# Two score units per TensorE mode switch, q and k transposes in two groups of four banks, q and k loaded by head halves

## The chip, the cores and the metric

The kernel runs on one core of one Trainium2 chip. The metric is the device time of one execution in microseconds (us), as the median of several runs. Before the change it is 365.46 us (364.68 to 366.66, 4 runs). Runs of one kernel differ by some tenths of a per cent, those of the changed kernel and some of its variants by up to 1.5%; a verdict "faster" or "slower" is given beyond 2%.

## The reference

Eight batches of attention with eight heads, 576 positions and head width 64, in a causal window of 128 with a linear position bias, followed by a two-layer network over all 4608 tokens:

```python
scores = q @ k.T / sqrt(64)                    # per batch and head
bias   = -slope[h] * |i - j|;  mask = (0 <= i - j < 128)
attn   = softmax(where(mask, scores + bias, -1e9))
x      = (attn @ v), heads side by side        # 4608 x 512
h      = x @ w_in                              # 512 -> 2048
out    = (h * cos(h)) @ w_out                  # 2048 -> 512, float32
```

## The kernel before

Everything is recorded in program order by a helper that derives the semaphore waits. Each engine runs its own list strictly in the order recorded. If TensorE's next instruction must wait, everything recorded behind it waits too.

The work is a chain of "chunks" of 512 tokens. For chunk c, TensorE does 16 groups of four first-layer matmuls (`moe1`; ScalarE makes the cosine, VectorE the product), with the q,k transposes of batch c+1 between them. Then comes the attention of batch c+1, whose chain over ScalarE and VectorE is long, so 64 second-layer matmuls of chunk c (`moe2_steps`) are dealt out between its pieces as filler.

```python
HB = [0, 1, 2, 3, 4, 5]                 # PSUM banks of the first layer; second layer: 6, 7
...
def qk_transposes(banks, engs):         # 8 steps: (half of the heads) x (q, k) x (two parts)
    ...                                 # one step: up to 10 transposes into one bank,
                                        # then one copy out of it, ScalarE or VectorE
...
def scores(b, u, n): banks = [2 * (n % 2), 2 * (n % 2) + 1]; ...   # keys 64 rows deep
def pv(b, u, n): ...                    # banks 4, 5; the tail unit "t" takes both
def norm(b, u, n): ...                  # VectorE: reciprocal, multiply
def x_back(b, u, n, eng): ...           # transposes the result back, eng copies it to xT
...
def attention(b, fill, plan):
    lead, part, last = plan
    take(lead)                          # take(n): n filler matmuls
    for j in range(2):
        scores(b, us[j], j)
        exps(b, us[j], j)
    mask(b, us[0])
    for j in range(n + 2):              # n = 9 units; unit 0 of batches 1..7 is the tail "t"
        take(part[0] if j < n else last)
        if 2 <= j:      x_back(b, us[j - 2], j - 2, "act")
        if j + 2 < n:   scores(b, us[j + 2], j + 2); exps(b, us[j + 2], j + 2)
        if j < n:       take(part[1]); pv(b, us[j], j)
        if j + 1 < n:   mask(b, us[j + 1])
        if j < n:       norm(b, us[j], j)
    for s in it: s()                    # what is left of the filler
...
for c in range(NCH):
    if c < B - 1:
        steps = iter(qk_transposes([6, 7], ["dve", "act"]))
        for fc in range(NFC):           # NFC = 16
            moe1(c, fc)
            if fc % 2 == 1:
                next(steps)()
        ...                             # loads of batch c + 2
        attention(c + 1, moe2_steps(c), (8, (2, 3), 3))
```

The transposes of q and k (64 columns wide, 128*64 in the traces), the scores and the tail's transposes back (64 rows deep, 64*128) use the array in halves; all other matmuls use all of it (128*128). "Mode switch" here means going from one to the other.

The softmax here doesn't subtract the row's maximum and nothing guards it: scores larger than these inputs give would overflow.

## Time and profile before

| | us |
|---|---|
| first-layer matmuls of chunk 0 begin (end of the prologue) | 30.62 |
| first period (chunk 0 to chunk 1) | 41.14 |
| each of the following six periods | 39.13 |
| the rest (last two chunks) | 58.76 |
| span of the profiled execution | 365.33 |

The first period is 2.0 us longer because of TensorE's clock. The trace records which share of the full clock was granted: here full from 14.61 us, half from 18.02 to 35.09, then full. Before its first record a trace says nothing, and views show full there; the distance between matmuls tells which clock it was.

The page of the kernel before, busy time by engine and then shares of the chain that ended last:

```profile
PE 341.4 (93%) x2912; PEld 164.6 (45%) x2912; DVE 233.1 (64%) x446; ACT 234.5 (64%) x352; POOL 61.3 (17%) x89
...
PE 79%; ACT 10%; DVE 6%; DMA 2%; issue 1%; POOL 1%; ACTq 0%; DVEq 0%; POOLq 0%
```

TensorE is busy 93% of the span and is 79% of the chain. So the question of any change is what TensorE does, and what it waits for.

The next lines are TensorE's timeline of the kernel before in the first-layer part of one period. Columns: start in us, length in us, engine, line of the program, operation, output and inputs, shapes, count. Lengths of matmuls overlap, since they are pipelined, so I read start to start.

```profile
71.77 1.89 PE L505 MATMUL ps<-xT,w_inb 128*128 128x512 bf16 x8
73.59 0.47 PE L290 MATMUL ps<-ident,qrows 128*64 128x128 bf16 x10
73.99 1.90 PE L505 MATMUL ps<-xT,w_inb 128*128 128x512 bf16 x8
```

Eight first-layer matmuls take 1.82 us until the transposes begin, where eight at the steady 0.216 us take 1.73: the entry costs 0.09. From matmul to matmul in the trace, the last full matmul before a transpose takes 0.309 us instead of 0.216, the first gap between two pairs of transposes 0.077 instead of 0.053, and the last transpose before a full matmul 0.151 instead of 0.056. One pair of switches costs about 0.21 us. A period has 16 pairs.

The same view at the start of the attention. L528 is the filler, L333 the tail scores, L342 the other scores:

```profile
89.40 1.90 PE L528 MATMUL ps<-w_outb,gT 128*128 128x512 bf16 x8
91.23 0.41 PE L333 MATMUL ps<-qt,kt 64*128 64x64 bf16 x16
91.48 0.33 PE L342 MATMUL ps<-qt,kt 64*128 64x256 bf16 x4
91.74 0.60 PE L528 MATMUL ps<-w_outb,gT 128*128 128x512 bf16 x2
92.96 0.39 PE L342 MATMUL ps<-qt,kt 64*128 64x256 bf16 x6 [0.62 <-ACT ptail L357]
```

The eight leading filler matmuls stand before the first scores. The third score unit waits 0.62 us, at 92.96, for the tail's exponential to free its banks.

TensorE's waits in the whole execution. Columns: engine, output, line, what it waited for; then us in total, times, longest:

```profile
PE ps L342 <- ACT ptail L357: 4.4, 7, 0.6
```

This line is that wait, once in each of seven periods. All waits of a period together are about 1.0 us.

### The profile page before, as it was taken

Reading aid. Unit: us, or ns where it says so; the run is one execution under the profiler, and the core shown is the slowest. Engines: PE = TensorE matmul, PEld = TensorE weight load, DVE = VectorE, ACT = ScalarE, POOL = GpSimd, SP = SyncE. Lnnn points to the kernel's source line nnn. Section 1 sums busy time; section 2 is a strip of 40 time slices with the busy share of each in tenths; the row PEclk is TensorE's granted clock in tenths of the full one; section 3 lists DMA queues with packets and bytes.
Section 4 is the critical chain, followed back from the end, with each engine's and each line's share of the span. In section 5 each row is a group of like instructions: output and inputs, shape, how many; then the busy total and the mean of one; then the engine's idle time right before and its main releaser. Section 6 shows DMA issues by size and latency. Waiting matters only on the chain.

```text
span 365.3 us, 7057 instructions
## 1 busy us (share of the span) xinstructions
PE 341.4 (93%) x2912; PEld 164.6 (45%) x2912; DVE 233.1 (64%) x446; ACT 234.5 (64%) x352; POOL 61.3 (17%) x89
## 2 busy tenths in 40 slices
PE   0688999999999999999999999999999999999996
PEld 0453445544454445444544455444544454444442
DVE  1683767577666766675857676776657675754431
ACT  5684786577757786678657875777567765843400
POOL 8860051003400150006000420015000000000000
PEclk9955999999999999999999999999999999999999
DMA  7999979105910193109910691039110011001012
GB/s 114 183 207 206 142 107 125 54 29 66 158 59 31 22 160 75 57 2 135 118 59 0 82 144 58 31 51 160 47 55 0 0 59 60 0 4 56 29 59 86
DMA packets 55648, 28.25 MB, mean 77 GB/s; under 512 B 38720, under 2 KB 51008, under 8 KB 55616
## 3 DMA queue, kind: packets, MB, share of 16 engines
q0 software_dynamic: 50432, 18.36, 44.8%
q1 hardware_dynamic: 5184, 9.44, 6.9%
q8 instruction: 23, 0.38, 0.4%
q14 instruction: 9, 0.07, 0.1%
HBM read 36.70 MB, written 9.44 MB: 126 GB/s over the span
## 4 chain that ended last, share of the span: by engine, by line
PE 79%; ACT 10%; DVE 6%; DMA 2%; issue 1%; POOL 1%; ACTq 0%; DVEq 0%; POOLq 0%
PE ps L505 33%; PE ps L528 30%; PE ps L290 5%; PE ps L342 5%; ACT cos L511 3%; ACT L357 2%; DMA krows<-in_k_dram 2%; PE ps L414 2%; ACT ptail L357 2%; PE ps L473 2%; PE ps L417 1%; ACT kt L303 1%; DVE kt L306 1%; DVE ob L533 1%; DVE gT L514 1%; DVE p L380 1%
## 5 line engine op out<-in xcount | busy, mean ns | idle before, releaser
L528 PE MATMUL ps<-w_outb,gT 128*128 128x512 bf16 x576 | 151.4, 380 | 0.0
L505 PE MATMUL ps<-xT,w_inb 128*128 128x512 bf16 x576 | 138.5, 384 | 0.2 <-ACT xT L487 0.2
L511 ACT ACTIVATE cos<-ps,halfpi 128x512 f32<-128x512 f32 x144 | 98.9, 688 | 52.2 <-PE ps L505 47.7
L514 DVE TENSOR_TENSOR gT<-ps,cos 128x512 bf16<-128x512 f32 x144 | 99.5, 692 | 50.7 <-ACT cos L511 50.7
L505 PEld LDWEIGHTS ps<-xT,w_inb 128*128 128x128 bf16 x576 | 52.6, 98 | 62.2 <-issue 2.4
L528 PEld LDWEIGHTS ps<-w_outb,gT 128*128 128x128 bf16 x576 | 45.6, 97 | 39.6 <-issue 4.4
L366 ACT ACTIVATE p<-ps 128x768 bf16<-128x768 f32 (+1 forms) x64 | 57.6, 915 | 6.2 <-PE ps L342 6.2
L487 ACT ACTIVATE xT<-ps 128x256 bf16<-128x256 bf16 (+3 forms) x80 | 28.9, 363 | 48.5 <-PE ps L473 42.8
L533 DVE COPY ob<-ps 128x512 f32<-128x512 f32 x36 | 24.9, 691 | 34.4 <-PE ps L528 34.4
L380 DVE TENSOR_TENSOR p<-p,emask 128x768 bf16<-128x768 bf16 (+1 forms) x64 | 39.5, 616 | 1.1 <-ACT p L366 0.9
L210 POOL DMA_DIRECT2D qrows<-in_q_dram x16 | 10.1, 640 | 172.4 <-PE ps L290 171.6
L218 POOL DMA_DIRECT2D vp<-in_v_dram x40 | 34.0, 888 | 0.0
L342 PE MATMUL ps<-qt,kt 64*128 64x128 bf16 (+1 forms) x320 | 24.6, 248 | 5.4 <-ACT ptail L357 4.4
L444 DVE TENSOR_TENSOR xnat<-ps,rec 128x256 bf16<-128x256 f32 x64 | 27.2, 425 | 2.2
L414 PEld LDWEIGHTS ps<-vp,p 128*128 128x128 bf16 x256 | 18.3, 100 | 17.4 <-ACT xT L487 8.4
L414 PE MATMUL ps<-vp,p 128*128 128x65 bf16 x256 | 23.1, 198 | 2.2 <-DVE rec L443 0.8
L290 PE MATMUL ps<-ident,qrows 128*64 128x128 bf16 x288 | 15.0, 239 | 8.8 <-DMA qrows<-in_q_dram 8.8
L417 PE MATMUL ps<-vp,p 128*128 128x65 bf16 x192 | 21.1, 198 | 0.0
L473 PE MATMUL ps<-ident,xnat 128*128 128x128 bf16 x128 | 18.6, 230 | 1.4 <-DVE xtail L435 1.2
L290 PEld LDWEIGHTS ps<-ident,qrows 128*64 128x64 bf16 x288 | 10.0, 119 | 21.0 <-issue 12.3
L473 PEld LDWEIGHTS ps<-ident,xnat 128*128 128x128 bf16 x128 | 12.3, 101 | 14.9 <-DVE xtail L435 1.4
L342 PEld LDWEIGHTS ps<-qt,kt 64*128 64x128 bf16 x320 | 11.4, 96 | 16.4 <-ACT ptail L357 7.8
(42 smaller groups left out, 196.7 us busy)
## 6 DMA issues: line engine op xcount, KB each, us to landing
out_dram<-ob SPq DMA_DIRECT2D x36, 256.0 KB, 2.0
qrows<-in_q_dram POOLq DMA_DIRECT2D x16, 288.0 KB, 5.0
krows<-in_k_dram POOLq DMA_DIRECT2D x16, 288.0 KB, 5.1
vp<-in_v_dram POOLq DMA_DIRECT2D x32, 128.0 KB, 6.3
w_inb<-in_moe_w_in_dram POOLq DMA_DIRECT2D x4, 512.0 KB, 10.6
w_outb<-in_moe_w_out_dram POOLq DMA_DIRECT2D x4, 512.0 KB, 19.9
vp<-in_v_dram POOLq DMA_DIRECT2D x8, 64.0 KB, 5.7
```

What stands on the lines that cost most here:

```text
L218: op("pool", lambda e, t=t, rows=rows: e.dma_start(vp[b % 2][0:rows, t, :, 0:64], v[b, :, 128 * t:128 * t + rows, :].rearrange("h p d -> p ...
L290: ins = e.transpose(dst[64 * x:64 * x + 64, 128 * (j - j0):128 * (j - j0) + 128], qB[which][:, 2 * pl + x, 64 * j:64 * j + 64], ident[:, :])
L342: ins = e.matmul(ps[:, banks[x], c0:c1], keys_ap(x, pr, kc), query_ap(x, pr, qb, 128 * nb), start=True, stop=True)
L366: op("act", lambda e: e.activation(P[i][:, :, lo:512], ps[:, 2 * slot:2 * slot + 2, lo:512], ACTF.Exp, scale=0.125), w=[("B", 2 * slot), ( ...
L380: op("dve", lambda e: e.tensor_tensor(P[i][:, :, lo:512], P[i][:, :, lo:512], EM[:, 2 * pr:2 * pr + 2, lo:512], ALU.mult), r=[("P", i), (" ...
L414: ins = e.matmul(o, P[i][:, x, d0:d0 + 128], V[:, kc, h, 0:65], start=True, stop=not two)
L473: ins = e.transpose(dst[:, 128 * r:128 * r + 128], xnat[n % NX][:, 128 * r:128 * r + 128], ident[:, :])
L487: op("act", lambda e, o=o, i=i: e.activation(o, i, ACTF.Copy), w=[("B", bank)] + keys)
L505: ins = e.matmul(ps[:, bank, :], w_in[:, kc, 128 * fc:128 * fc + 128], xT[:, kc, r0:r0 + CH], start=(kc == 0), stop=(kc == NPAIR - 1))
L511: op("act", lambda e: e.activation(cosb[ci][:, :], ps[:, bank, :], ACTF.Sin, bias=halfpi[:, 0:1]), r=["halfpi"], w=[("B", bank), ("cos", ci)])
L514: op("dve", lambda e: e.tensor_tensor(gT[gi][:, fc, :], ps[:, bank, :], cosb[ci][:, :], ALU.mult), r=[("cos", ci)], w=[("B", bank), ("g", ...
L528: op("pe", lambda e: e.matmul(ps[:, bank, :], gT[gi][:, fc, 128 * t:128 * t + 128], w_out[:, fc, :], start=(fc == 0), stop=(fc == NFC - 1) ...
```

## The change

The intent is to save mode switches. The eight transpose groups of a batch become two groups of four banks, two score units are computed in one visit, the PSUM banks are dealt out anew for that (four instead of six for the first layer), and q and k come in halves of the heads, so that work on the first batch can begin earlier.

```diff
-        HB = [0, 1, 2, 3, 4, 5]
+        HB, SB, UB, OB = [0, 1, 2, 3], [4, 5, 6, 7], [2, 3], [0, 1]
     # first layer; scores and transposes; value products; second layer
...
-        def load_qk(which, src, b):
+        def load_qk(which, src, b, pl):        # one half of the heads
...
-        def attention(b, fill, plan):
+        def attention(b, fill, plan, x_eng):
+            ng = (n + 1) // 2                  # groups of two units
+            for j in members(0): scores(b, us[j], j)
+            for j in members(0): exps(b, us[j], j)
+            for j in members(0): mask(b, us[j])
+            for g in range(ng + 1):
+                before, after, between = plan(g)
+                take(before)
+                for j in members(g - 1): x_back(b, us[j], j, x_eng(j))
+                for j in members(g + 1): scores(b, us[j], j)
+                for j in members(g + 1): exps(b, us[j], j)
+                take(after)
+                ahead = list(members(g + 1))
+                for i, j in enumerate(members(g)):
+                    if i: take(between)
+                    pv(b, us[j], j); norm(b, us[j], j)
+                    if i < len(ahead): mask(b, us[ahead[i]])
...
-                steps = iter(qk_transposes([6, 7], ["dve", "act"]))
+                group = [qk_transposes(pl, SB, ["act", "dve", "act", "dve"]) for pl in range(2)]
                 for fc in range(NFC):
                     moe1(c, fc)
-                    if fc % 2 == 1:
-                        next(steps)()
+                    for pl in range(2):
+                        if fc == 1 + 7 * pl:
+                            for tp, cp in group[pl]: tp()      # transposes only
+                        elif fc in [3 + 7 * pl, 4 + 7 * pl, 6 + 7 * pl, 7 + 7 * pl]:
+                            group[pl].pop(0)[1]()          # one copy
...
-                attention(c + 1, moe2_steps(c), (8, (2, 3), 3))
+                attention(c + 1, moe2_steps(c),
+                          lambda g: ((20, 4, 3), (5, 3, 3), (5, 3, 3), (5, 3, 3), (5, 1, 0),
+                                     (4, 0, 0))[g], lambda j: "act")
```

At the 2nd and 9th first-layer group four banks of transposes are issued, and their copies follow one by one in the `elif` branch. In the first batch the change transposes the first half of the heads before the attention and the second half inside it. Not shown: the first batch takes its units in another order and has VectorE make every fourth copy of `x_back`, and there are four buffers for the exponentials instead of three.

More of the change, by code (lines that the diff above doesn't have):

```diff
@@ L177, in bass_alibi_sliding__then__act_gcu_kernel @@
         EMt = sb("emtail", [128, H, 128])
-        NP = 3
+        NP = 4
         P = [sb(f"p{i}", [128, 2, 512]) for i in range(NP)]
@@ L210, in load_qk @@
                 fns.append(lambda e, g=g: e.dma_start(
-                    qB[which][64 * g:64 * g + 64, :, :],
-                    src[b, 4 * g:4 * g + 4, :, :].rearrange("h (s j) d -> s h (j d)", j=9)))
-            op("pool", fns, w=[("qB", which)], dma=f"ld{which}")
+                    qB[which][64 * g:64 * g + 64, 2 * pl:2 * pl + 2, :],
+                    src[b, 4 * g + 2 * pl:4 * g + 2 * pl + 2, :, :].rearrange(
+                        "h (s j) d -> s h (j d)", j=9)))
+            op("pool", fns, w=[("qB", which, pl)], dma=f"ld{which}{pl}")
         def load_v(b, order=range(NBLK)):
@@ L271, in masks, with qk_transposes @@
                    r=[("EM", h) for h in range(x, H, 2)], w=["EMt"])
-        def qk_transposes(banks, engs):
+        def qk_transposes(pl, banks, engs):
             out_ = []
             n = 0
-            for pl in range(2):
-                for which in ("q", "k"):
-                    for (j0, j1) in ((0, 5), (5, 9)):
-                        def step(pl=pl, which=which, j0=j0, j1=j1, n=n):
-                            bank = banks[n % len(banks)]
-                            nj = j1 - j0
-                            dst = ps[:, bank, :].bitcast(BF16)[:, 0:nj * 128]
-                            def tp(e):
-                                ins = None
-                                for j in range(j0, j1):
-                                    for x in range(2):
-                                        ins = e.transpose(
-                                            dst[64 * x:64 * x + 64,
-                                                128 * (j - j0):128 * (j - j0) + 128],
-                                            qB[which][:, 2 * pl + x, 64 * j:64 * j + 64],
-                                            ident[:, :])
-                                return ins
-                            op("pe", tp, r=[("qB", which), "ident"], w=[("B", bank)])
-                            o = tr[which][:, :].rearrange("p (g l t) -> p g l t", g=2, l=2)[
-                                :, :, pl, 0:576].rearrange("p g (s j) -> p g s j", j=9)[
-                                :, :, :, j0:j1]
-                            i = dst.rearrange("p (j g s) -> p g s j", j=nj, g=2)
-                            key = ("tr", which, pl, j0)
-                            if engs[n % len(engs)] == "act":
-                                op("act", lambda e: e.activation(o, i, ACTF.Copy),
-                                   w=[("B", bank), key])
-                            else:
-                                op("dve", lambda e: e.tensor_copy(o, i), w=[("B", bank), key])
-                        out_.append(step)
-                        n += 1
@@ new lines, in qk_transposes, with tp, f, cp @@
+            for which in ("q", "k"):
+                for (j0, j1) in ((0, 5), (5, 9)):
+                    bank = banks[n % len(banks)]
+                    nj = j1 - j0
+                    dst = ps[:, bank, :].bitcast(BF16)[:, 0:nj * 128]
+                    def tp(which=which, j0=j0, j1=j1, bank=bank, dst=dst):
+                        def f(e):
+                            ins = None
+                            for j in range(j0, j1):
+                                for x in range(2):
+                                    ins = e.transpose(
+                                        dst[64 * x:64 * x + 64,
+                                            128 * (j - j0):128 * (j - j0) + 128],
+                                        qB[which][:, 2 * pl + x, 64 * j:64 * j + 64],
+                                        ident[:, :])
+                            return ins
+                        op("pe", f, r=[("qB", which, pl), "ident"], w=[("B", bank)])
+                    def cp(which=which, j0=j0, j1=j1, nj=nj, bank=bank, dst=dst, eng=engs[n]):
+                        o = tr[which][:, :].rearrange("p (g l t) -> p g l t", g=2, l=2)[
+                            :, :, pl, 0:576].rearrange("p g (s j) -> p g s j", j=9)[
+                            :, :, :, j0:j1]
+                        i = dst.rearrange("p (j g s) -> p g s j", j=nj, g=2)
+                        key = ("tr", which, pl, j0)
+                        if eng == "act":
+                            op("act", lambda e: e.activation(o, i, ACTF.Copy),
+                               w=[("B", bank), key])
+                        else:
+                            op("dve", lambda e: e.tensor_copy(o, i), w=[("B", bank), key])
+                    out_.append((tp, cp))
+                    n += 1
@@ L318, in units @@
             if b == 0:
-                return [(pr, G) for G in range(2) for pr in (0, 2, 1, 3)] + [("t", None)]
+                return [(pr, G) for p0 in range(2) for G in range(2) for pr in (p0, p0 + 2)] + [
+                    ("t", None)]
             return [("t", None)] + [(pr, G) for pr in range(NPAIR) for G in range(2)]
@@ L323, in scores @@
             slot = n % 2
-            banks = [2 * slot, 2 * slot + 1]
+            banks = SB[2 * slot:2 * slot + 2]
             def f(e):
@@ L352, in exps @@
             slot = n % 2
+            banks = SB[2 * slot:2 * slot + 2]
+            held = [("B", x) for x in banks]
+            src_ = ps[:, banks[0]:banks[0] + 2, :]
             if u[0] == "t":
@@ L357, in exps @@
                 op("act", lambda e: e.activation(
-                    Pt[i][:, 0:1024], ps[:, 2 * slot:2 * slot + 2, :].rearrange("p a b -> p (a b)"),
-                    ACTF.Exp, scale=0.125),
-                   w=[("B", 2 * slot), ("B", 2 * slot + 1), ("Pt", i)])
+                    Pt[i][:, 0:1024], src_.rearrange("p a b -> p (a b)"), ACTF.Exp, scale=0.125),
+                   w=held + [("Pt", i)])
                 return
@@ L365, in exps @@
             lo = 0 if u[1] else 128
-            op("act", lambda e: e.activation(P[i][:, :, lo:512], ps[:, 2 * slot:2 * slot + 2, lo:512],
+            op("act", lambda e: e.activation(P[i][:, :, lo:512], src_[:, :, lo:512],
                                              ACTF.Exp, scale=0.125),
-               w=[("B", 2 * slot), ("B", 2 * slot + 1), ("P", i)])
+               w=held + [("P", i)])
         def mask(b, u):
@@ L384, in ubanks @@
         def ubanks(u, n):
-            return [4, 5] if u[0] == "t" else [4 + n % 2]
+            return UB if u[0] == "t" else [UB[n % 2]]
         def pv(b, u, n):
@@ L397, in f @@
                             h = 2 * pr + x
-                            o = ps[:, 4 + x, 65 * pr:65 * pr + 65]
+                            o = ps[:, UB[x], 65 * pr:65 * pr + 65]
                             c0 = 512 * x + 128 * pr
@@ L428, in norm @@
             if u[0] == "t":
-                U = ps[0:64, 4:6, 0:260].rearrange("p x (k c) -> p x k c", c=65)
+                U = ps[0:64, UB[0]:UB[0] + 2, 0:260].rearrange("p x (k c) -> p x k c", c=65)
                 rv = rc[0:64, 0:8].rearrange("p (x k) -> p x k", x=2)
@@ L432, in norm @@
                 op("dve", lambda e: e.reciprocal(rv, U[:, :, :, 64]),
-                   w=[("B", 4), ("B", 5), ("rec", n % 2)])
+                   w=[("B", UB[0]), ("B", UB[1]), ("rec", n % 2)])
                 for x in range(2):
@@ L437, in norm @@
                         rv[:, x, :, None].broadcast_to([64, 4, 64]), ALU.mult),
-                       r=[("rec", n % 2)], w=[("B", 4 + x), ("xtl",)])
+                       r=[("rec", n % 2)], w=[("B", UB[x]), ("xtl",)])
                 return
@@ L523, in moe2_steps @@
                 tg = 4 * c + t
-                bank = 6 + tg % 2
+                bank = (OB if c < B - 1 else SB)[tg % 2]
                 oi = tg % NOB
@@ L550, in take, with members @@
                         s()
-            lead, part, last = plan
             us = units(b)
             n = len(us)
-            take(lead)
-            for j in range(2):
+            ng = (n + 1) // 2
+            def members(g):
+                return range(2 * g, min(2 * g + 2, n)) if 0 <= g < ng else ()
+            for j in members(0):
                 scores(b, us[j], j)
+            for j in members(0):
                 exps(b, us[j], j)
-            mask(b, us[0])
-            for j in range(n + 2):
-                take(part[0] if j < n else last)
-                if 2 <= j:
-                    x_back(b, us[j - 2], j - 2, "act")
-                if j + 2 < n:
-                    scores(b, us[j + 2], j + 2)
-                    exps(b, us[j + 2], j + 2)
-                if j < n:
-                    take(part[1])
+            for j in members(0):
+                mask(b, us[j])
@@ new lines, in attention @@
+            for g in range(ng + 1):
+                before, after, between = plan(g)
+                take(before)
+                for j in members(g - 1):
+                    x_back(b, us[j], j, x_eng(j))
+                for j in members(g + 1):
+                    scores(b, us[j], j)
+                for j in members(g + 1):
+                    exps(b, us[j], j)
+                take(after)
+                ahead = list(members(g + 1))
+                for i, j in enumerate(members(g)):
+                    if i:
+                        take(between)
@@ L568, in attention @@
                     pv(b, us[j], j)
-                if j + 1 < n:
-                    mask(b, us[j + 1])
-                if j < n:
                     norm(b, us[j], j)
+                    if i < len(ahead):
+                        mask(b, us[ahead[i]])
+                for j in ahead[len(members(g)):]:
+                    mask(b, us[j])
             for s in it:
                 s()
-        load_qk("q", q, 0)
-        load_qk("k", k, 0)
-        constants()
+        for pl in range(2):
+            load_qk("q", q, 0, pl)
+            load_qk("k", k, 0, pl)
+            if pl == 0:
+                constants()
@@ L580, in bass_alibi_sliding__then__act_gcu_kernel @@
         load_v(0)
         masks()
-        for s in qk_transposes([4, 5, 6, 7], ["dve", "act"]):
-            s()
+        first = qk_transposes(0, UB + OB, ["dve", "act", "dve", "act"])
+        for tp, cp in first:
+            tp()
+            cp()
         for u in range(4):
             load_w_in(u)
-        load_qk("q", q, 1)
-        load_qk("k", k, 1)
+        load_qk("q", q, 1, 0)
+        load_qk("k", k, 1, 0)
+        attention(0, [lambda s=s: (s[0](), s[1]())
+                      for s in qk_transposes(1, OB + UB, ["dve", "act", "dve", "act"])],
+                  lambda g: (0, 2, 2) if g == 0 else (0, 0, 0),
+                  lambda j: "dve" if j % 4 == 3 else "act")
@@ L588, in bass_alibi_sliding__then__act_gcu_kernel @@
+        load_qk("q", q, 1, 1)
+        load_qk("k", k, 1, 1)
         for u in range(4):
             load_w_out(u)
-        load_v(1)
-        attention(0, [], (0, (0, 0), 0))
+        load_v(1, (3, 4, 0, 1, 2))
         for c in range(NCH):
             if c < B - 1:
-                steps = iter(qk_transposes([6, 7], ["dve", "act"]))
+                group = [qk_transposes(pl, SB, ["act", "dve", "act", "dve"]) for pl in range(2)]
                 for fc in range(NFC):
                     moe1(c, fc)
-                    if fc % 2 == 1:
-                        next(steps)()
+                    for pl in range(2):
+                        if fc == 1 + 7 * pl:
+                            for tp, cp in group[pl]:
+                                tp()
+                        elif fc in [3 + 7 * pl, 4 + 7 * pl, 6 + 7 * pl, 7 + 7 * pl]:
+                            group[pl].pop(0)[1]()
@@ L599, in bass_alibi_sliding__then__act_gcu_kernel @@
                 if c + 2 < B:
-                    load_qk("q", q, c + 2)
-                    load_qk("k", k, c + 2)
+                    for pl in range(2):
+                        load_qk("q", q, c + 2, pl)
+                        load_qk("k", k, c + 2, pl)
                     load_v(c + 2)
-                attention(c + 1, moe2_steps(c), (8, (2, 3), 3))
+                attention(c + 1, moe2_steps(c),
+                          lambda g: ((20, 4, 3), (5, 3, 3), (5, 3, 3), (5, 3, 3), (5, 1, 0),
+                                     (4, 0, 0))[g], lambda j: "act")
```

## The prediction

> **What bounds the kernel now.** TensorE issue. The page has PE 93% busy (DVE 64%, ACT 64%); the chain of waits is 79% PE. The timeline shows seven equal periods of 39.1 us (71.77 to 110.91), one per batch: 17.6 us of first-layer matmuls with the q,k transposes between them, 21.5 us of attention filled with 64 second-layer matmuls. A 512-column matmul issues every 0.216 us. Real PE waits in a period are only about 1.0 us: 0.69 for the first tail exponential (after a 1.28 us table load on ACT), 0.33 at a value product.
>
> **What a mode switch costs (PE timeline, start to start).** A full matmul before a 64-wide one: 0.309 us instead of 0.216; the first gap inside the group 0.077 instead of 0.053; leaving, 0.151 instead of 0.056. About 0.21 us a pair. The Trainium skill ("TensorEngine Tiling (Array Packing)", Key Properties) says that changing the tiling mode drains the engine; the trace agrees. Pairs per period: 16 before (8 transpose groups, 8 score visits), 8 after (2 and 6: a full-array transpose now separates the 64-row tail transpose from the scores). Saved: 8 x 0.21 = 1.7 us. If both old waits vanish too: 2.7 us a period, a floor near 36.4.
>
> **What the change adds.** New PE waits in each period, since PE is in order:
> - A. The second transpose group (after matmul group 8) needs its last bank, freed by a DVE copy queued behind the product of group 7. Matmuls begin to product ended is 2.47 us, copy 0.8: about 1.0 us wait.
> - B. The scores of the first two units now come before the lead of second-layer matmuls (before: 8 matmuls, 1.7 us, first). The tail unit needs the last key copy, on DVE behind the product of group 14: free about 3.3 to 3.8 us after that group began, PE arrives at 1.8. Wait 1.5 to 2.0 us.
> - C. The filler plan asks for 70 matmuls of 64. With 20 in the lead, nothing is left after the third-last step: the last unit's product waits for ACT's copy out of its bank (about 0.6), its transpose back for reciprocal and multiply (0.85), and in three of seven periods the next first-layer matmul for the last copy (0.8).
> - E. The tail unit holds both value banks; its normalization takes 1.1 to 1.3 us on DVE, but only 3 matmuls (0.65) stand before the next unit's product: about 0.7.
> - D. Transposes back: 5 matmuls (1.08 us) against a chain of 1.2: 0.4 together.
> Four first-layer banks suffice: a bank is held 2.5 us, reused after 3.46.
>
> Sum: 5.5 to 6 us of waits against 2.7 saved, about +3 us a period, +21 in seven.
>
> **Prologue.** ACT's masks end at 9.6 us and DVE's tail mask at 10.2, so half loads landing earlier save only to there: first scores at about 12 instead of 14.8. First-layer matmuls start 2 to 3 us earlier than 30.6. The last 59 us unchanged.
>
> **Prediction: 383 us, range 369 to 397.** Chances: faster by over 2% 0.07, within 2% 0.11, slower by over 2% 0.82.
>
> **Right or wrong.** Right: half as many 0.309/0.151 gaps, periods near 42 us, PE waits at the places of A to E. Wrong: periods of 37 to 38 us without them: then I misread what covers them.
> **Other risk.** The PE clock was halved (18.0 to 35.1 us) where PE worked thinly; waits B and C might trip this in each period, costing more.

## More of the kernel before

Where the interval of a ratio straddles that limit, the verdict is "unclear".

## The result, and the profile after

The changed kernel takes 397.84 us (393.44 to 398.77, 4 runs). The ratio to the kernel before is 1.086, with a 95% interval of 1.077 to 1.095: slower. Ratios here are the mean time of one kernel's fast runs over that of the other's of the same rounds, so they are not quite the ratio of the medians quoted.

| us | before | after | difference |
|---|---|---|---|
| prologue | 30.62 | 33.94 | +3.3 |
| seven periods together | 275.9 | 298.7 | +22.8 |
| of these, each late period | 39.13 | 42.10 | +3.0 |
| the rest | 58.76 | 58.78 | 0 |
| span of the profiled execution | 365.3 | 391.4 | +26.1 |

The prologue of the changed kernel ran at half clock throughout: the clock records begin at 37.24 us with full clock, and until then first-layer matmuls stand 0.427 us apart instead of 0.216. That of the kernel before had full clock for 3.4 us and then half, so the +3.3 compares nearly, but not quite, the same clock. Half clock until 37.24 also lengthens the first period here (44.37 us; the next two take 43.16 and 42.76).

The page of the changed kernel, the same two lines:

```profile
PE 337.0 (86%) x2912; PEld 169.8 (43%) x2912; DVE 225.9 (58%) x448; ACT 225.7 (58%) x350; POOL 79.6 (20%) x121
...
PE 66%; DVE 18%; ACT 11%; issue 4%; POOL 1%; ACTq 0%; POOLq 0%; DVEq 0%
```

TensorE is busy a little less in all, 337.0 instead of 341.4 us, over a longer span. Its share of the chain fell from 79% to 66%, and VectorE's rose from 6% to 18%. TensorE did not get more work; it waits more.

TensorE's waits of the changed kernel, with the columns as before:

```profile
PE ps L336 <- DVE kt L308: 12.5, 7, 1.8
PE ps L478 <- DVE xnat L449: 12.1, 21, 0.8
...
PE ps L290 <- DVE kt L308: 5.6, 7, 0.8
PE ps L419 <- DVE xtail L440: 4.4, 7, 0.6
...
PE ps L510 <- ACT xT L492: 1.6, 3, 0.7
```

All five are new or longer than before. The three lines with a count of seven happen once in each period. Of the 21 waits on `DVE xnat`, seven (3.7 us) lie in the first batch's attention and two in each period. The last line is of the first three periods only. I call the waits by the letters of the prediction.

TensorE's timeline of the changed kernel in the first-layer part of a period (L510 first layer, L290 transposes). Wait A is the one at 217.20:

```profile
206.34 1.89 PE L510 MATMUL ps<-xT,w_inb 128*128 128x512 bf16 x8
208.16 0.69 PE L290 MATMUL ps<-ident,qrows 128*64 128x128 bf16 x18
208.68 0.67 PE L290 MATMUL ps<-ident,krows 128*64 128x128 bf16 x18
209.28 6.22 PE L510 MATMUL ps<-xT,w_inb 128*128 128x512 bf16 x28
215.43 0.69 PE L290 MATMUL ps<-ident,qrows 128*64 128x128 bf16 x18
215.96 0.45 PE L290 MATMUL ps<-ident,krows 128*64 128x128 bf16 x10
217.20 0.41 PE L290 MATMUL ps<-ident,krows 128*64 128x128 bf16 x8 [0.80 <-DVE kt L308]
217.55 1.68 PE L510 MATMUL ps<-xT,w_inb 128*128 128x512 bf16 x7
```

Each visit now transposes four banks at one switch. But the last eight transposes of the second visit wait 0.80 us (0.96 start to start above the normal gap) for a VectorE copy (`kt L308`): it frees the bank that the first visit used last, and on VectorE it stands behind the product of group 7.

The same view at the start of the attention, with waits B and E (L336 tail scores, L533 filler, L419 value products):

```profile
221.23 2.54 PE L510 MATMUL ps<-xT,w_inb 128*128 128x512 bf16 x11
225.55 0.41 PE L336 MATMUL ps<-qt,kt 64*128 64x64 bf16 x16 [1.79 <-DVE kt L308]
225.78 0.35 PE L345 MATMUL ps<-qt,kt 64*128 64x256 bf16 x4
226.06 4.49 PE L533 MATMUL ps<-w_outb,gT 128*128 128x512 bf16 x20
...
232.34 0.81 PE L533 MATMUL ps<-w_outb,gT 128*128 128x512 bf16 x3
233.78 0.25 PE L419 MATMUL ps<-vp,p 128*128 128x65 bf16 x3 [0.63 <-DVE xtail L440]
```

B: the tail scores come right after the first-layer matmuls and wait 1.79 us for the last copy of the transposed keys. E: the value product at 233.78 waits 0.63 us for the tail unit's normalization, because the tail holds both value banks. In the kernel before, five filler matmuls and a score unit stood between these two.

The end of the same batch, with wait C (L478 transposes back; two rows of the last value product are shown, at 247.16 and 247.38):

```profile
245.54 1.03 PE L533 MATMUL ps<-w_outb,gT 128*128 128x512 bf16 x4
246.41 0.64 PE L478 MATMUL ps<-ident,xnat 128*128 128x128 bf16 x4
247.16 0.20 PE L419 MATMUL ps<-vp,p 128*128 128x65 bf16 x1
...
247.38 0.19 PE L422 MATMUL ps<-vp,p 128*128 128x65 bf16 x1
248.31 0.29 PE L478 MATMUL ps<-ident,xnat 128*128 128x128 bf16 x2 [0.74 <-DVE xnat L449]
248.44 1.24 PE L510 MATMUL ps<-xT,w_inb 128*128 128x512 bf16 x5
```

All 64 filler matmuls are gone at 246.4. From there to the next chunk at 248.44, TensorE has only fourteen short transposes and matmuls in 2 us. It waits about 0.3 us before the last value product and 0.9 us after it. D is the rest of the waits on `DVE xnat`: at 243.27 the second transpose back of a middle group comes 0.63 us late, at 246.77 another 0.24.

From the start-to-start gaps of this late period (206.34 to 248.44) the sum is A 0.96, B 1.86, C 1.17, D 0.87, E 0.80, together 5.7 us. Without them the period would be 36.4 us. The mode switches are saved as planned: counted in the traces, a late period has 8 pairs instead of 16 (at the q,k transposes 2 entries instead of 8, with 0.309 us each). The saving is simply smaller than the waits.

### The profile page after: what moved, and what is told of

It is laid out like the page before. It is cut to its first block, busy times and chain, and to the rows that moved or that the text cites. A ratio compares the mean times of both kernels' runs of the same rounds, so it can differ in the third digit from the quotient of the medians.

```text
span 391.4 us, 7083 instructions
## 1 busy us (share of the span) xinstructions
PE 337.0 (86%) x2912; PEld 169.8 (43%) x2912; DVE 225.9 (58%) x448; ACT 225.7 (58%) x350; POOL 79.6 (20%) x121
## 4 chain that ended last, share of the span: by engine, by line
PE 66%; DVE 18%; ACT 11%; issue 4%; POOL 1%; ACTq 0%; POOLq 0%; DVEq 0%
PE ps L533 28%; PE ps L510 21%; ACT cos L516 7%; DVE gT L519 5%; PE ps L345 4%; PE ps L290 3%; DVE xnat L449 3%; PE ps L419 3%; PE ps L478 3%; DVE kt L308 2%; DVE xtail L440 2%; DVE p L385 1%; PE ps L422 1%; DVE qt L308 1%; DVE ob L538 1%
## 5 line engine op out<-in xcount | busy, mean ns | idle before, releaser
L533 PE MATMUL ps<-w_outb,gT 128*128 128x512 bf16 x576 | 142.3, 380 | 0.0
L510 PE MATMUL ps<-xT,w_inb 128*128 128x512 bf16 x576 | 132.3, 383 | 1.6 <-ACT xT L492 1.6
L516 ACT ACTIVATE cos<-ps,halfpi 128x512 f32<-128x512 f32 x144 | 95.4, 688 | 49.0 <-PE ps L510 45.8
L510 PEld LDWEIGHTS ps<-xT,w_inb 128*128 128x128 bf16 x576 | 54.9, 98 | 67.4 <-ACT xT L492 2.1
L533 PEld LDWEIGHTS ps<-w_outb,gT 128*128 128x128 bf16 x576 | 49.5, 97 | 51.7 <-issue 4.4
L210 POOL DMA_DIRECT2D qrows<-in_q_dram x32 | 19.7, 630 | 182.9 <-PE ps L290 182.1
L448 DVE RECIPROCAL rec<-ps 128x4 f32<-128x4 f32 x64 | 11.5, 180 | 33.0 <-PE ps L422 32.9
L478 PE MATMUL ps<-ident,xnat 128*128 128x128 bf16 x128 | 18.0, 233 | 12.6 <-DVE xnat L449 12.1
L419 PE MATMUL ps<-vp,p 128*128 128x65 bf16 x256 | 23.1, 200 | 6.2 <-DVE xtail L440 4.4
L419 PEld LDWEIGHTS ps<-vp,p 128*128 128x128 bf16 x256 | 19.0, 101 | 19.1 <-issue 8.4
L345 PE MATMUL ps<-qt,kt 64*128 64x128 bf16 (+1 forms) x320 | 20.8, 253 | 3.3 <-DVE kt L308 2.6
L210 POOL DMA_DIRECT2D krows<-in_k_dram x32 | 19.6, 636 | 2.6 <-issue 2.6
L290 PE MATMUL ps<-ident,krows 128*64 128x128 bf16 x288 | 13.1, 232 | 7.1 <-DVE kt L308 5.6
L478 PEld LDWEIGHTS ps<-ident,xnat 128*128 128x128 bf16 x128 | 9.2, 99 | 23.0 <-DVE xnat L449 17.4
```

The source lines that it names most:

```text
L210: fns.append(lambda e, g=g: e.dma_start(qB[which][64 * g:64 * g + 64, 2 * pl:2 * pl + 2, :], src[b, 4 * g + 2 * pl:4 * g + 2 * pl + 2, :, ...
L345: ins = e.matmul(ps[:, banks[x], c0:c1], keys_ap(x, pr, kc), query_ap(x, pr, qb, 128 * nb), start=True, stop=True)
L419: ins = e.matmul(o, P[i][:, x, d0:d0 + 128], V[:, kc, h, 0:65], start=True, stop=not two)
L478: ins = e.transpose(dst[:, 128 * r:128 * r + 128], xnat[n % NX][:, 128 * r:128 * r + 128], ident[:, :])
L510: ins = e.matmul(ps[:, bank, :], w_in[:, kc, 128 * fc:128 * fc + 128], xT[:, kc, r0:r0 + CH], start=(kc == 0), stop=(kc == NPAIR - 1))
L516: op("act", lambda e: e.activation(cosb[ci][:, :], ps[:, bank, :], ACTF.Sin, bias=halfpi[:, 0:1]), r=["halfpi"], w=[("B", bank), ("cos", ci)])
```

## The experiments

The theory is the prediction's: TensorE waits at places A to E, which come from the order of the program. One rival is that the vector engines' chain sets the period, so moving filler only moves the idle time. Another is that the first layer suffers from four instead of six banks. For the prologue, the rivals are the half loads, the transposes moved into the first attention, and the pairing of units. "Later period" below is the one that repeats from the fourth period on, read in the profiled execution; it differs by some hundredths between repeats, so it separates causes better than whole times do. (In four runs one or more of the periods from the fourth on are longer: up to 1.6 us in `tail_second` and `all_transposes_first`, which is the clock again, see the end, and 0.2 in `combined` and `four_halves_lead_ten`.) The column "first layer begins" is less steady: the six runs with the first attention of the kernel before (named `before...` and `four...`) differ in it by up to 1.8 us, with clock records that differ too. `four_and_halves` and `four_halves_lead_ten` have the same prologue program and differ by 0.6.

| run | median us (range) | ratio to before | first layer begins | later period |
|---|---|---|---|---|
| before | 365.46 (364.68 to 366.66) | | 30.62 | 39.13 |
| the change | 397.84 (393.44 to 398.77) | 1.086 | 33.94 | 42.10 |
| `lead_first` | 382.32 (381.68 to 382.82) | 1.045 | 33.95 | 40.38 |
| `short_lead` | 383.65 (383.04 to 384.07) | 1.049 | 33.95 | 41.00 |
| `copies_earlier` | 382.32 (381.55 to 382.69) | 1.045 | 33.95 | 40.40 |
| `tail_second` | 394.51 (391.00 to 396.75) | 1.078 | 33.95 | 41.80 |
| `all_transposes_first` | 395.44 (394.76 to 397.69) | 1.083 | 33.21 | 42.11 |
| `first_unit_by_unit` | 392.20 (389.14 to 394.40) | 1.071 | 30.02 | 42.11 |
| `before_four_banks` | 365.95 (365.42 to 366.31) | 1.000 | 30.12 | 39.13 |
| `before_two_per_visit` | 357.99 (357.50 to 359.43) | 0.979 | 28.99 | 38.06 |
| `combined` | 358.80 (357.92 to 358.99) | 0.981 | 29.94 | 37.73 |
| `before_four_per_visit` | 355.07 (354.17 to 355.65) | 0.970 | 29.88 | 37.60 |
| `four_and_halves` | 355.66 (353.70 to 356.72) | 0.971 | 29.44 | 37.60 |
| `four_halves_lead_ten` | 353.98 (352.74 to 354.63) | 0.967 | 28.82 | 37.24 |

All twelve gave correct results.

### lead_first: wait B alone

```diff
+            take(lead)                          # lead = 8
             for j in members(0): scores(b, us[j], j)
-   plan (20, 4, 3), ...
+   plan (12, 4, 3), ...
```

> The changed kernel, but 8 of the 20 leading second-layer matmuls stand before the first two score units of a batch instead of behind them; all else equal. Theory (in-order waits of TensorE at named places): the wait for the last key copy ahead of the tail scores, 1.86 us a period, shrinks to at most 0.3; periods of the later batches go from 42.1 to about 40.5 us; whole kernel about 11 us faster than the change, near 386. Rival (the chain over ScalarE and VectorE sets the period, so filler moved on TensorE only shifts the idle time): the period stays within 0.5 us of 42.1.

The later period was 40.38 us, 1.72 less than the change's. The gap before the tail scores fell from 2.17 us to 0.45 start to start, where 0.31 is the bare switch. So B was real idle time, and eight filler matmuls that were there all along fill it. The rival, that the vector chain sets the period, fails here. The whole kernel gained more, 15.5 us instead of the 12 that seven periods make. So did `short_lead` and `copies_earlier` (14.2 and 15.5 us, where I expected 9 and 12). Against the profiled run of the change (393.44 us), their profiled runs are 9.9 and 11.4 us faster, as the periods say; for the rest the clock is the likely cause, see the end.

### short_lead: wait C alone

```diff
-   plan (20, 4, 3), ...
+   plan (10, 4, 3), ...
```

> The changed kernel with 10 leading second-layer matmuls instead of 20, one number; the plan then asks for 60 of the 64, so matmuls are left for the end of the batch. Theory: the wait of the last transpose back for its normalization (0.93 us) and the part of the wait before the last value product go, and in the three early periods also the wait of the first-layer matmuls for the last copy (0.7); no new wait at the start, since about 8 to 9 matmuls cover the first two exponentials. Later periods from 42.1 to about 41.0, early ones 1.8 us shorter; whole kernel about 9 us faster, near 388. Rival (vector chain sets the period, or the lead of 20 covers something I missed): period unchanged or longer.

The later period was 41.00, as expected, and the early ones were shortened to 40.9 and 41.0 (from 43.16 and 42.76). TensorE's waits of this run, the two lines that answer to the first two of the change:

```profile
PE ps L336 <- DVE kt L308: 12.6, 7, 1.8
PE ps L478 <- DVE xnat L449: 6.9, 14, 0.8
```

B is untouched (12.6 against 12.5 us), while the waits on `DVE xnat` fell from 12.1 us in 21 places to 6.9 in 14: one place in each period went. A lead of 20 was not needed at the start, where with 10 the list of waits has none that the change did not have, and matmuls were missing at the end.

### copies_earlier: waits A and B through their cause

```diff
-  elif fc in [3 + 7 * pl, 4 + 7 * pl, 6 + 7 * pl, 7 + 7 * pl]:
+  elif fc in [2 + 7 * pl, 3 + 7 * pl, 5 + 7 * pl, 6 + 7 * pl]:
```

> The changed kernel with each of the eight copies of transposed q and k one first-layer group earlier (one constant, 3 to 2). Theory: the wait of the second transpose group for the last copy of the first (0.96 us) falls to about 0.1, the wait before the tail scores from 1.86 to about 1.0; period 42.1 to about 40.4; whole kernel about 12 us faster, near 386. Rival (ScalarE and VectorE saturated in this stage, four banks): copies earlier only push the cosine and product chain back, TensorE waits for banks, period within 0.5 us of 42.1.

The later period was 40.40, as expected. The first two lines of TensorE's waits that matter here:

```profile
PE ps L478 <- DVE xnat L449: 12.0, 21, 0.8
PE ps L336 <- ACT cos L516: 6.5, 7, 0.9
```

The line of A (`PE ps L290 <- DVE kt`) is no longer among the long waits. B is now 6.5 us in seven places, 0.9 each, and is put down to ScalarE. One first-layer group is 0.86 us, which is what B lost (1.79 to 0.93 us of idle time); the period fell by 1.70, the two waits together.

### tail_second: wait E, mostly a miss

```diff
-  return [("t", None)] + [(pr, G) for pr in range(NPAIR) for G in range(2)]
+  us = [(pr, G) for pr in range(NPAIR) for G in range(2)]
+  return us[:1] + [("t", None)] + us[1:]
```

> The changed kernel with the tail unit as second unit of a batch instead of first. Theory: the 0.8 us that the second value product waits for the tail's normalization falls to about 0.2 (the tail's product waits for one short normalization instead), and the tail transposes back now stand next to the scores, so one mode switch pair (0.2 us) goes; period 42.1 to about 41.3; whole kernel about 5 us faster, near 392. Rival: unchanged.

The later period was 41.80: 0.3 us less, not 0.8. E fell from 0.80 to 0.34 us start to start, and one mode switch pair went (7 instead of 8), but another wait took their place. TensorE's waits of this run:

```profile
PE ps L465 <- ACT xT L493: 3.5, 7, 0.7
```

This line is new, 0.5 us in each period. L465 is the tail's transpose back. It writes into the first value bank, the same that unit 0's transpose back has just filled, so it waits for ScalarE to copy that out (`xT L493`). I had looked at the normalization and not at the bank. A tail that transposes back into its other bank should avoid it; this was not run.

### all_transposes_first and first_unit_by_unit: the prologue

```diff
   # all_transposes_first
-  for tp, cp in first:
+  for tp, cp in first + qk_transposes(1, UB + OB, ["dve", "act", "dve", "act"]):
       tp()
       cp()
-  attention(0, [second half's transposes as filler], ...)
+  attention(0, [], ...)
   # first_unit_by_unit: the same, and the first attention in the loop of the kernel before
+  attention0(0)
```

> The changed kernel, but the first batch's second four transpose groups stand before its attention as in the kernel before; loads still by head halves, score units still in pairs. It tells apart why the first first-layer matmul comes at 33.95 us instead of 30.6. If the transposes inside the first attention cost it (they take TensorE, ScalarE and VectorE in its middle and share banks with the value products): first-layer matmuls start near 31.5. If the pairing does (no filler matmuls in this batch, so TensorE, ScalarE and VectorE wait for each other pair by pair): still near 33. Whole kernel 0 to 3 us faster than the change.

> As the run with all transposes first, and the first batch's attention in the order of the kernel before (unit by unit, scores two units ahead). Loads still by head halves. Theory: the start of the first-layer matmuls returns to 29 to 30.6 us (30.6 before; the halves may give up to 1.5 us back), so 3.3 to 5 us less than the change's 33.95; periods later unchanged at 42.1. Rival (the half loads and their longer issue on GpSimd delay the start): stays above 32.

Taking the second half's transposes out of the first attention moved the start of the first layer from 33.94 to 33.21 us. Taking the pairing out as well moved it to 30.02. So of 3.9 us, 3.2 are the pairing (with it went the copies on VectorE, whose own share was not tested). In all three traces the first-layer matmuls still stand 0.427 us apart at that point, so the clock was half in each and is not the difference. Nor are the half loads, which all three have. TensorE's waits between 14 and 34 us, first in the changed kernel, then in `all_transposes_first`, then in `first_unit_by_unit`:

```profile
PE ps L478 <- DVE xnat L449: 3.7, 7, 0.8
PE ps L464 <- DVE xtail L440: 1.2, 1, 1.2
```

```profile
PE ps L478 <- DVE xnat L449: 4.3, 8, 0.8
```

```profile
PE ps L419 <- ACT xT L492: 1.3, 3, 0.6
PE ps L478 <- DVE xtail L440: 1.2, 1, 1.2
```

The first batch has no filler. In pairs, TensorE waits for nearly each normalization (3.7 us in seven places, 4.3 in eight with all transposes first), then does two transposes back and two scores, and ScalarE waits in turn. Unit by unit, these waits of the transposes back on `xnat` are gone, and fewer and shorter ones remain.

### before_four_banks: the rival of the banks

```diff
-        HB = [0, 1, 2, 3, 4, 5]
+        HB = [0, 1, 2, 3]
```

> The kernel before with four instead of six banks for the first layer, nothing else: tests whether the change lost time to the smaller number of banks. Theory: same within 0.5% of 365.5, periods 39.1 (a bank is held 2.5 us and needed again after 3.46). Rival (fewer banks throttle the first layer): periods of 40 to 42, kernel 5% slower.

The ratio was 1.000 (0.998 to 1.002), with periods of 39.13. The smaller number of banks cost nothing.

### before_two_per_visit: the gain by itself

```diff
-                    if fc % 2 == 1:
-                        next(steps)()
+                    if fc % 4 == 1:
+                        group = [next(steps) for _ in range(2)]
+                        for tp, cp in group: tp()
+                        for tp, cp in group: cp()
```

> The kernel before with the eight q,k transpose groups of a batch in four visits of two banks (banks 6 and 7, which it has already), after first-layer groups 1, 5, 9 and 13; nothing of the lead, the scores or the loads is touched. Measures the gain of fewer mode switches by itself. Theory: four switch pairs of 0.21 us less in each of seven periods and no new wait: periods 39.13 to about 38.3, kernel about 6 us faster, near 359.5 (1.6%). Rival (a switch's cost is hidden by something else, or the two copies at once hold the banks up): periods stay at 39.1.

The period fell by 1.07 us to 38.06, and the kernel was 2.1% faster (0.976 to 0.982 of the kernel before: "unclear" by the limit of 2%, but clear of noise). Four switch pairs at 0.21 us make 0.85 of the period's gain. The last copy now comes earlier too, and the wait at the third score unit fell by 0.20 (from 1.00 to 0.80 us start to start). The idea of the change is sound; its cost was in the placing.

### combined: the change with its repairs

The edit joins `lead_first` (5 ahead of the scores, 13 behind), `copies_earlier`, `tail_second`, `first_unit_by_unit`, and this plan, which sums to 64:

```diff
-   (20, 4, 3), (5, 3, 3), (5, 3, 3), (5, 3, 3), (5, 1, 0), (4, 0, 0)
+   (13, 3, 4), (6, 2, 3), (5, 2, 3), (5, 2, 3), (3, 1, 0), (4, 0, 0)    # lead = 5
```

> The changed kernel with the repairs together: copies one group earlier, 5 second-layer matmuls before the first scores and 13 behind them (18 are what ScalarE's table load and two exponentials need), tail unit second, filler plan that sums to 64, first batch unit by unit with all its transposes first. Theory: the mode switches saved stay saved and the waits mostly go; later periods 37.2 to 37.8 us, first-layer matmuls start near 30, whole kernel 353 to 358, faster than the kernel before by 2 to 3.5%. Rival (fewer filler matmuls than the chain needs, so that waits only change places): periods stay above 39.

It took 358.80 us, 39 less than the change and 1.9% less than the kernel before (0.979 to 0.983 of it, so "unclear" by the limit of 2%). The later period is 37.73, as expected; the whole is 0.8 us above my range. The first three periods (39.95, 38.64, 38.38) are longer: each ends with a wait of about 0.5 us for the last copy of a batch, and the first ran at half clock until 33.83 us. What is left includes the 0.5 us at the tail's transpose back.

### before_four_per_visit: the transposes alone, placed well

```diff
-        HB = [0, 1, 2, 3, 4, 5]
+        HB = [0, 1, 2, 3]
...
+                steps = qk_transposes([6, 7, 4, 5], ["dve", "act"])
                 for fc in range(NFC):
                     moe1(c, fc)
+                    g4 = fc // 8
+                    if fc % 8 == 1:
+                        for tp, cp in steps[4 * g4:4 * g4 + 4]: tp()
+                    elif 2 <= fc % 8 <= 5:
+                        steps[4 * g4 + fc % 8 - 2][1]()
```

> The kernel before, with its own attention order, leads and loads, four first-layer banks (shown to cost nothing) and the q,k transposes in two visits of four banks as in the change, but visits after groups 1 and 9 and the copies in the four groups that follow each, so that no group waits for the copies of the other. Theory: six switch pairs of 0.21 us less than the kernel before and the second wait at the scores a little shorter: periods 37.4 to 37.7, whole kernel near 354.5 (3% faster). Rival (visits of four stall in any placing, as in the change): slower than the run with two per visit, 358.

It took 355.07 us, 3.0% less than the kernel before, with a period of 37.60. The timeline of TensorE at the two visits (L508 first layer, L290 transposes; this trace lacks some matmul records, hence counts such as x31 and the 0.16 us of "issue"):

```profile
144.40 1.89 PE L508 MATMUL ps<-xT,w_inb 128*128 128x512 bf16 x8
146.22 0.69 PE L290 MATMUL ps<-ident,qrows 128*64 128x128 bf16 x18
146.74 0.67 PE L290 MATMUL ps<-ident,krows 128*64 128x128 bf16 x18
147.57 6.85 PE L508 MATMUL ps<-xT,w_inb 128*128 128x512 bf16 x31 [0.16 <-issue]
154.35 0.69 PE L290 MATMUL ps<-ident,qrows 128*64 128x128 bf16 x18
154.88 0.67 PE L290 MATMUL ps<-ident,krows 128*64 128x128 bf16 x18
```

Both visits run through, 36 transposes in about 1.2 us, with no wait for a copy. With the scores still one unit per visit, this beats `combined`. That kernel has 7 pairs of switches in a late period where this one has 10, which at 0.21 us saves 0.6 us, but it waits at its transposes back (0.64, 0.46 and 0.24 us start to start). As placed there, the pairing of scores brought nothing on top; a placing without these waits was not run.

### four_and_halves and four_halves_lead_ten

`four_and_halves` adds the loads by head halves of the change to `before_four_per_visit`. `four_halves_lead_ten` then changes one number:

```diff
-  attention(c + 1, moe2_steps(c), (8, (2, 3), 3))
+  attention(c + 1, moe2_steps(c), (10, (2, 3), 3))
```

> The kernel before with four transpose groups per visit (355.07), and in addition the loads of q and k by head halves as in the change, nothing else: the third part of the change by itself. Theory: transposes start near 6 us instead of 8.8, but the masks hold the copies to about 9.5, so the first scores come at about 13.4 instead of 14.8 and the first-layer matmuls 0.5 to 1.4 us before 29.9; periods stay at 37.6; whole kernel about 354. Rival (the halves' extra issues delay other loads): first-layer matmuls at 30 or later, kernel 355 or more.

> As the run with four per visit and halves, with 10 instead of 8 second-layer matmuls before the first scores. Theory: the remaining wait of 0.52 us a period before the third score unit (for the tail's exponential, behind the table load) falls to about 0.1, since table load and exponential do not start later; periods 37.6 to about 37.2, kernel about 3 us faster, near 351. Rival (the exponential waits for the scores, so all shifts by 0.43 us): periods 37.6.

The half loads by themselves: the transposes began at 5.94 us instead of 6.68 in `before_four_per_visit`, but the first scores at 13.65 against 13.66. (In the profile of the kernel before they began at 14.80; there q landed 2.1 us later, with the same loads.) The first layer began at 29.44 against 29.88 in single profiles, and the medians are 355.66 and 355.07. So no gain of the half loads is seen, and my "about 354" missed. The early first scores of the change (11.65 us) come from leaving half of the transposes for later: with all of them first they began at 13.66 there too.

The longer lead gave 37.24 per period and 353.98 us, the fastest of all, 3.3% below the kernel before, though not the 351 that I had expected. The size per period (0.36 us) came near my 0.4, but the place was wrong. The waits of TensorE for the tail's exponential, first in `before_four_per_visit` (the total is the same in `four_and_halves`), then here:

```profile
PE ps L345 <- ACT ptail L360: 3.1, 7, 0.5
```

```profile
PE ps L346 <- ACT ptail L361: 2.9, 7, 0.4
```

That wait stayed nearly the same. What went is the 0.33 us that one value product of each period waited after its filler, which is 0.55 us start to start in the one trace and 0.22 in the other. Why the exponential did not come earlier relative to the scores is open.

## Why the prediction was right or wrong

- **The periods were right.** Predicted about +3 us each, near 42; measured 42.10 against 39.13. Over seven: +21 predicted, +22.8 measured, since each of the first three is 3.2 to 4.0 us longer than that of the kernel before.
- **The gain of fewer switches was right.** Predicted floor without waits 36.4 us; from the gaps, 36.4. `before_two_per_visit` and `before_four_per_visit` show the gain alone: 1.07 and 1.53 us a period.
- **Waits A to E were at the places predicted.** A 1.0 predicted, 0.96 measured; B 1.5 to 2.0, measured 1.86; C 1.45 in late periods (0.6 and 0.85), measured 1.17; D 0.4, measured 0.87; E 0.7, measured 0.80. The sum, 5.7 us, fell into the predicted 5.5 to 6 partly because C came out smaller and D larger. `lead_first`, `short_lead` and `copies_earlier` each took one or two of them away, or most of one, and the period fell by the amount. E was only exchanged for another wait, and D was not tested by itself.
- **Four banks suffice: right**, by `before_four_banks`.
- **The prologue was wrong in sign.** The step that failed is "First-layer matmuls start 2 to 3 us earlier than 30.6": they start 3.3 us later. The first scores did come earlier (11.65 us, I had said about 12), but that lead of 3.1 us over the kernel before (14.80) was lost in the first attention. I counted the engines' work and overlooked that pairs without filler make the engines wait for each other. `first_unit_by_unit` and `all_transposes_first` put 3.2 us on that and 0.7 on the transposes in the middle.
- **The clock, named as a risk and not counted, was real.** In the traces of `tail_second`, `lead_first` and `all_transposes_first`, some periods have a stretch of 3.4 us in which the granted clock is half. The windows of `tail_second` before, in and after one, with columns of busy us and counts for PE, PEld, DVE, ACT, POOL, then granted clock, DMA share and GB/s:

```profile
74.90:78.40 3.50, 2.10 (x20) 1.00 (x18) 2.00 (x6) 1.47 (x4) 0.00 (x0) 1.00 0.20 75
78.40:81.80 3.40, 3.40 (x16) 1.21 (x16) 0.69 (x1) 1.95 (x3) 0.00 (x0) 0.50 0.00 0
81.80:85.20 3.40, 3.40 (x44) 1.97 (x41) 1.38 (x2) 1.55 (x3) 2.38 (x4) 1.00 0.33 40
```

The six stretches in these traces begin 0.2 to 0.9 us after wait C ends, and the work that pays is the next first-layer matmuls; 3.4 us at half clock cost 1.7. The third period of `lead_first` has one and took 42.64 us, 1.6 more than the 41.04 that the change's third period less 1.72 gives. The profiled run of the change has none after its prologue (span 391.4; its mean clock of 1.0 covers only what was recorded, from 37.24 us on). Its other runs have spans of 395.2, 397.1 and 396.8 at mean clocks of 0.991, 0.987 and 0.987. Twice 0.013 of 397 us is 10 us, the length of three such stretches, as in `tail_second` with the same mean clock; by the same sum 0.991 is two. Two and three stretches would cost 3.4 and 5.1 us, and these spans are 3.8, 5.7 and 5.4 longer. That these three runs had them in the same places is inferred from the mean clock, not seen, as they left no trace. `short_lead`, in which most of C is gone, had mean clocks of 0.998 or more and varied by only 1 us; but the same holds for `copies_earlier`, which keeps C. Exactly what trips the clock is therefore not settled.

So the predicted 383 us was 15 too low at the median, which lies 0.8 us above the range's end. Of these 15, 5.8 are the prologue (+3.3 instead of -2.5) and 1.8 the periods (22.8 instead of 21). Most of the rest lies between profiled runs and medians: the change's profiled run took 393.44 us, 4.4 less than its median, for which the clock is the likely cause, and the profiled run of the kernel before took 367.24, 1.8 more than its median.

## What to carry to other kernels

When instructions run in order, grouping work to save a fixed cost moves every wait of the group to one place: ask for each group what its last buffer or last copy waits for, and whether independent work still stands in front of it. Filler is a budget: here a plan that asked for 70 of 64 matmuls spent them at the start and left the end of each batch bare, and placing them right (1.72 us a period in `lead_first`, 1.10 in `short_lead`) was worth more than the mode switches (1.7). Take one part of such a change by itself, in the order that the kernel already has; here four transpose banks per visit with copies spaced out gave 3% where the whole change cost 9%.

## What the Trainium skill lacked or had wrong

- "TensorEngine Tiling (Array Packing)", Key Properties, says that switching the tiling mode drains TensorE, and gives no cost. The runs show it: 0.093 us more at the entry, 0.024 in the first gap inside, 0.095 at the exit, 0.21 us a pair at full clock.
- "TensorE: Matmul & The Clock Gate", Part 1, ties the fall to the half clock to an idle window of about 3.4 us, and the table near its end asks for no idle gaps over about 3 us. Under a second failure mode, Part 1 adds that frequent small idles between groups of matmuls can make the clock swing too, without saying how small. Here the clock fell after 3.5 us in which TensorE still counted 2.1 us busy and no single wait of TensorE was over 1 us (`tail_second`, 74.9 to 78.4); the same thin stretch of other periods and runs did not always do it. The length of the stretch at half clock, 3.4 us, agrees with the page's window.
- The same page, Part 4, says that full clock does not engage for transposes. In the kernel before, full clock was granted at 14.6 us, when TensorE had run nothing but q,k transposes, and their start-to-start gap had been 0.106 us until then, against 0.053 in the later periods. `before_four_per_visit` shows the same at 13.61 us. Whether these transposes run in the mode that the page means, the trace does not say.
